# Cached-attention decode step: K and V loaded by whole batches of a cache head, score tiles of four batches in turn

## The chip, the cores and the metric

The kernel runs on one NeuronCore of one Trainium2 chip. The metric is device time in microseconds (us) of one execution; smaller is better. The kernel before was timed in three runs: median 1330.52 us, from 1330.09 to 1330.75. A further execution was profiled, and every row shown below comes from it.

## The reference

A decode step for 8 batches, one new token each, is the sum of three parts: the input `x`, attention over a long key and value cache, and a dense layer with the Mish activation. All data is float32.

```python
xn = layernorm(x)                                   # x: 8 x 512
q  = (xn @ wq) as 32 query heads of 128             # wq: 512 x 4096
s  = q . k_cache / sqrt(128)                        # k_cache: 8 batches x 8 heads x 8192 keys x 128
p  = softmax(s)                                     # 4 query heads share one cache head
o  = p . v_cache                                    # v_cache: the same shape as k_cache
A  = o @ wo                                         # wo: 4096 x 512
Bp = mish(xn @ w1 + b1) @ w2                        # w1: 512 x 1792, w2: 1792 x 512
out = x + A + Bp
```

The K cache and the V cache have 268.4 MB each. The four weights add 24.1 MB, so each execution reads 561 MB once, and nothing of it is used twice.

## The kernel before, in words

**Layout.** The host lays K and V out in blocks of 1024 keys, 512 KiB each, so that eight consecutive blocks hold the 8192 keys of one (batch, cache head). A K block is stored with the head dimension outermost, 128 rows of 1024 keys; a V block is stored so that each partition gets 1024 consecutive elements.

**Units.** Work on the cache goes by units of four blocks (`G` = 4), which is half of the keys of one (batch, head): 2 MiB. A unit is one DMA from the SyncE queue (`load_unit`, L94 to L101) into one of eight buffers named `kv` (L79, L85). The unit is read as 128 consecutive pieces, one for each partition, so each partition receives one contiguous row of 16 KiB. For K such a row is four consecutive head-dimension elements of one block: partition p holds block p // 32. Head 0 is loaded differently (L106 to L113), in rows of 8 KiB, two a partition, so that its query operand is smaller and ready sooner.

**Scores.** `scores` (L254 to L274) multiplies a K unit with a block-diagonal query operand `qT`: 128 columns, which are four blocks by 32 (4 query heads times 8 batches), with zeros outside the unit's own batch and block. The units of all eight batches accumulate into one PSUM tile of 128 x 1024, `S[0]` for the first half of the keys and `S[1]` for the second (L137). A unit takes eight matrix products of 128 x 128 by 512 columns, each of which the profile shows as two MATMUL records because the data is float32. After a half's last batch VectorE takes the row maximum (L272).

**Softmax and values.** After both halves of a head `maximum` (L278) and `weights` (L292) turn the maximum into a bias, ScalarE exponentiates each half out of PSUM (L303) and VectorE transposes it into `pt` (L304). `sums` (L314) adds up the row sums. `values` (L321) multiplies `pt` with V units, 16 columns wide, into one of two PSUM tiles `O`; after the second unit of a batch VectorE folds the result into `os` with four instructions (L337, L339), and `merge` (L350) sums over partitions with a small product. `outputs` (L363) multiplies a head's result with its part of `wo`.

**Projections.** A `wq` tile serves two heads: `project` (L201) makes the queries, scales and repeats them on VectorE (L219), transposes them four times on TensorE (L225) and copies them into `qc` (L228); `expand` (L235) writes `qc` into the block-diagonal `qT` with 16 small copies (L250).

**Order.** One list of items, `items` (L502 to L525), fixes the order: `wq`, then K units alone for the first head, then K units of head n+1 and V units of head n in turn, `wq` and `wo` tiles between them, and at the end 16 V units alone, the last `wo` tile and three `w2` tiles. The loop at L528 issues the load of the item that is six ahead (`AHEAD`), then the work of the present one. A load waits on the SyncE queue until its buffer is free. Small steps (softmax, merge, outputs) are put off by a count of items with `after` (L453), so that TensorE has other work while VectorE or ScalarE prepare them. The last of these, `outputs` of the last head, is put off by 0, so it is issued with the `wo` tile and before the `w2` tiles.

Of the kernel before, what the change touches and what calls it, by code (L numbers as in the profile page):

```python
# [8 lines left out]
F32 = mybir.dt.float32  # L9
# [16 lines left out]
UK = SK // NH  # L26
GK = UK // G
# [10 lines left out]
R = B * REP  # L38
PU = NH * B
# [4 lines left out]
KR = DH // Q  # L44
# [12 lines left out]
BUFS = 8  # L57
AHEAD = 6
# [3 lines left out]
def kernel(  # L62
# [21 lines left out]
    def buffer():  # L84
        return kv.tile([P, G * BW], F32, name="kv")  # L85
# [8 lines left out]
    def load_unit(src, n, b, s):  # L94

        lo = ((b * HKV + n) * NH + s) * G
        t = buffer()
        nc.sync.dma_start(
            t, src[lo : lo + G].rearrange("j p f -> (j p f)").rearrange("(p f) -> p f", p=P)
        )  # L100
        return t  # L101

    def load_k(n, b, s):
        if n > 0:
            return load_unit(kT, n, b, s)
        lo = ((b * HKV + n) * NH + s) * G  # L106
# [9 lines left out]
    def load_v(n, b, s):  # L116

        return load_unit(v, n, b, s)
# [18 lines left out]
    S = [psum.tile([P, GK], F32, name=f"s{i}") for i in range(NH)]  # L137
# [8 lines left out]

    rsel = const.tile([P, R], F32, name="rsel")

# [3 lines left out]
    qT = [const.tile([P, B * (QB + 1)], F32, name=f"qT{i}") for i in range(QBUFS)]  # L152
    qc = const.tile([P, HKV, KR, REP, B], F32, name="qc")
# [4 lines left out]
    def setup():  # L158
# [10 lines left out]
        scratch = work.tile([P, NH, GK], F32, name="e", bufs=1)  # L169
        xc, sq = scratch[:B, 0, :D], scratch[:B, 1, :D]  # L170
# [23 lines left out]
        )  # L194
        nc.vector.reduce_sum(rsel, ident.rearrange("p (g r) -> p r g", g=G), axis=AX.X)
        used = rsel[:, : W4 * REP]
        nc.vector.reduce_sum(hsel, used.rearrange("p (i h) -> p h i", h=REP), axis=AX.X)
        nc.vector.reduce_sum(isel, used.rearrange("p (i h) -> p i h", h=REP), axis=AX.X)


    def project(n, w):  # L201

        for c in range(CC):
            for h in range(REP):
                lo = (n % 2 * REP + h) * DH
                nc.tensor.matmul(  # L206
                    H[Q * h : Q * h + B, 384:512],
                    xnT[:, c, :],
                    w[:, c, lo : lo + DH],
                    start=(c == 0),  # L210
                    stop=(c == CC - 1),
                )

        k = KR if n > 0 else KA
        qs = work.tile([P, KR, P], F32, name="qs", bufs=1)[:, :k, :].rearrange(
            "p r (g i) -> p r g i", g=k
        )
        for g in range(k):
            nc.vector.tensor_scalar_mul(  # L219
                qs[:, :, g, :],  # L220
                H[:, 384:512].rearrange("p (i r) -> p r i", r=k),
                DH**-0.5,
            )
        for i in range(k):
            nc.tensor.transpose(  # L225
                H[:, i * P : (i + 1) * P], qs[:, i].rearrange("p g i -> p (g i)"), ident
            )
        nc.vector.tensor_copy(  # L228
            qc[:, n, :k],
            H[:, : k * P].rearrange("p (r h q) -> p r h q", r=k, h=REP)[:, :, :, :B],  # L230
        )

    Q0 = []

    def expand(n):  # L235

        if n > 0:
            k, cols, t = KR, P, qT[n % QBUFS]
        else:

            k, cols, t = KA, WK, work.tile([P, NH, W * R], F32, name="pt")
            t = t.rearrange("p s w -> p (s w)")[:, : B * (QA + 1)]
            nc.gpsimd.memset(t, 0.0)
            Q0.append(t)
        t = t.rearrange("p (b c) -> p c b", b=B)
        for g in range(k):
            rows = slice(P // k * g, P // k * (g + 1))
            for i in range(k):
                lo = i * cols + g * R
                nc.vector.tensor_copy(t[rows, lo : lo + R : B, :], qc[rows, n, i])  # L250

    NM = {}

    def scores(n, b, s, k):  # L254

        k_rows, cols, pitch, t = (KR, P, QB, qT[n % QBUFS]) if n > 0 else (KA, WK, QA, Q0[0])
        for c in range(GK // 512):
            for i in range(k_rows):
                w = pitch * b + cols * i
                at = i * BW + c * 512  # L260
                for j in range(P // cols):
                    nc.tensor.matmul(  # L262
                        S[s][cols * j : cols * (j + 1), c * 512 : (c + 1) * 512],
                        t[:, w : w + cols],
                        k[:, at : at + 512] if n > 0 else k[:, j, at : at + 512],
                        start=(b == 0 and i == 0),
                        stop=(b == B - 1 and i == k_rows - 1),
                    )
        if b == B - 1:
            if s == 0:  # L270
                NM[n] = work.tile([P, NH], F32, name="nm")
            nc.vector.tensor_reduce(  # L272
                NM[n][:, s : s + 1], S[s], axis=AX.X, op=ALU.max, negate=True
            )  # L274
# [3 lines left out]
    def maximum(n):  # L278

        nmb = work.tile([P, 1], F32, name="nmb")  # L280
        nc.vector.tensor_reduce(nmb, NM[n], axis=AX.X, op=ALU.min)
        nc.tensor.transpose(M[:1, 0:P], nmb, ident)
        nr = work.tile([1, Q], F32, name="nr")
# [3 lines left out]
        nx = NX[n] = work.tile([1, G, Q], F32, name="nx")  # L287
        nc.vector.tensor_copy(
            nx, nr.rearrange("p (o q) -> p o q", o=1).to_broadcast([1, G, Q])
        )  # L290

    def weights(n):  # L292


        nc.tensor.transpose(M[:, 128:129], NX[n].rearrange("p g q -> p (g q)"), ident[:1, :1])
        nmx = work.tile([P, 1], F32, name="nmx")
        nc.vector.tensor_copy(nmx, M[:, 128:129])  # L297
        e = work.tile([P, NH, GK], F32, name="e", bufs=1)
        l = work.tile([P, NH], F32, name="l")
        pt = PT[n] = work.tile([P, NH, W * R], F32, name="pt")  # L300
        m = W // TG
        for s in range(NH):
            nc.scalar.activation(e[:, s], S[s], AF.Exp, bias=nmx, accum_out=l[:, s : s + 1])  # L303
            nc.vector.transpose(  # L304
                pt[:, s].rearrange("p (m t r) -> p t m r", m=m, t=TG),
                e[:, s].rearrange("p (t q m) -> p t m q", t=TG, m=m),
            )
        ls = work.tile([P, 1], F32, name="ls")
        nc.vector.reduce_sum(ls, l, axis=AX.X)
        lsel = work.tile([P, R], F32, name="lsel")  # L310
        nc.vector.tensor_scalar(lsel, rsel, ls, None, op0=ALU.mult)
        return lsel

    def sums(n, lsel):  # L314
        nc.tensor.matmul(M[:, 136 : 136 + R], ones, lsel, start=True, stop=True)  # L315
        RT[n] = work.tile([P, REP, B], F32, name="r")
        nc.vector.reciprocal(RT[n].rearrange("p h b -> p (h b)"), M[:, 136 : 136 + R])  # L317
# [3 lines left out]
    def values(n, b, s, vt):  # L321
# [3 lines left out]
        for k in range(W // W4 // G):  # L325
            for c in range(G):
                j = G * k + c
# [252 lines left out]
```

## Time and profile before

| | |
|---|---|
| median of three runs | 1330.52 us |
| profiled execution | 1331.33 us |
| its span, first to last instruction | 1329.2 us |
| HBM read in it | 561.01 MB, 422 GB/s over the span |
| TensorE busy (matmul) | 1185.3 us, 89% of the span |
| VectorE, ScalarE, GpSimd busy | 200.8, 23.7, 8.7 us |
| mean granted TensorE clock | 0.972 |

The span leaves out 2.1 us of the profiled execution, before its first and after its last instruction. Matrix products are pipelined and their ends are modelled, so the time that a product costs in a stream is best read from the starts of two successive groups and not from the mean duration of one record. In the chain of work that ended last, the profile follows the program back from its last instruction, at each step to whatever released it; a piece named after a DMA is the time between the issue of that DMA and its landing.

### The profile page before, as it was taken

To read this page: it belongs to the slowest core of one execution; us is meant where nothing else is said; L and a number is where in the kernel's file an instruction comes from. 1 tells how busy PE (TensorE), PEld (TensorE's weight loads), DVE (VectorE), ACT (ScalarE), POOL (GpSimd) and SP (SyncE) were. 2 spreads that over 40 slices of the span, in tenths; PEclk is the share of its full clock that TensorE was granted. 3 is DMA by queue.
4 is the path that set the end of the run, shared out by engine and by line. 5 is a ranking of instruction groups with operands and counts; after the bars stand their busy time and mean duration, and the time that the engine had idled before them with its cause. 6 is when DMAs were issued, how large, how long until landed. Compare 5 with 4: busy or idle time off the path is not lost.

```text
span 1329.2 us, 11146 instructions
## 1 busy us (share of the span) xinstructions
PE 1185.3 (89%) x4962; PEld 457.6 (34%) x4962; DVE 200.8 (15%) x549; ACT 23.7 (2%) x39; POOL 8.7 (1%) x10
## 2 busy tenths in 40 slices
PE   5878999989999998989999999999999999999756
PEld 1223333333333333333333333433333333333212
DVE  4302020120002002030010200203100020100311
ACT  1000000000000000000000000000000000000000
POOL 2000000000000000000000000000000000000000
PEclk9999999999999999999999999899999999999786
DMA  9999999999999999999999999999999999999997
GB/s 383 421 424 428 428 424 427 427 428 430 426 428 426 429 426 426 426 426 429 427 427 427 427 428 424 429 426 427 427 428 427 428 427 428 427 428 427 427 428 298
DMA packets 44903, 561.80 MB, mean 423 GB/s; under 512 B 4396, under 2 KB 4528, under 8 KB 9784
## 3 DMA queue, kind: packets, MB, share of 16 engines
q1 hardware_dynamic: 44832, 561.07, 99.7%
q8 instruction: 39, 0.64, 0.2%
q14 instruction: 8, 0.07, 0.0%
q10 hardware_dynamic: 24, 0.02, 0.0%
HBM read 561.01 MB, written 0.07 MB: 422 GB/s over the span
## 4 chain that ended last, share of the span: by engine, by line
DMA 55%; PE 40%; DVE 3%; ACT 1%; issue 0%; ACTq 0%
DMA kv<-in_kT 50%; PE s L262 32%; PE o L328 6%; DMA kv<-in_w 3%; DMA kv<-in_v 2%; ACT e L303 1%; DVE os L339 1%; PE m L376 1%; PE h L442 0%; DVE e L173 0%; DVE os L337 0%; DVE nm L272 0%; PE h L206 0%; PE m L352 0%; PE m L315 0%
## 5 line engine op out<-in xcount | busy, mean ns | idle before, releaser
L262 PE MATMUL s<-kv,qT 128*128 128x512 f32 x1792 | 809.1, 605 | 44.9 <-DMA kv<-in_kT 41.6
L262 PEld LDWEIGHTS s<-kv,qT 128*128 128x128 f32 x1792 | 335.5, 192 | 506.5 <-issue 407.0
L328 PE MATMUL o<-kv,pt 128*16 128x512 f32 x2048 | 268.3, 630 | 13.1 <-DMA kv<-in_v 10.7
L337 DVE TENSOR_SCALAR os<-o,isel 128x128 f32<-128x128 f32 x64 | 22.5, 351 | 745.3 <-PE o L328 745.3
L328 PEld LDWEIGHTS o<-kv,pt 128*16 128x16 f32 x2048 | 55.1, 114 | 164.4 <-issue 139.6
L262 PE MATMUL s<-kv,pt 128*64 128x512 f32 x256 | 60.6, 619 | 14.1 <-DMA kv<-in_kT 14.1
L339 DVE SCALAR_TENSOR_TENSOR os<-o,isel,os 128x128 f32<-128x128 f32 x192 | 67.2, 350 | 6.3
L272 DVE TENSOR_REDUCE nm<-s 128x1 f32<-128x1024 f32 x16 | 19.6, 1225 | 216.1 <-PE s L262 215.9
L352 PE MATMUL m<-hsel,os 128*128 128x4 f32 x128 | 21.1, 235 | 31.2 <-DVE os L339 31.2
L352 PEld LDWEIGHTS m<-hsel,os 128*128 128x128 f32 x128 | 22.7, 193 | 67.0 <-DVE os L339 47.9
L303 ACT ACTIVATE e<-s,nmx 128x1024 f32<-128x1024 f32 x16 | 17.7, 1109 | 1174.5 <-DVE nmx L297 1174.5
L262 PEld LDWEIGHTS s<-kv,pt 128*64 128x64 f32 x256 | 17.7, 141 | 57.4 <-issue 32.2
L304 DVE STREAM_TRANSPOSE pt<-e 128x1024 f32<-128x1024 f32 x16 | 31.3, 2000 | 1.4 <-ACT e L303 1.3
L250 DVE COPY qT<-qc 32x32 f32<-32x32 f32 x112 | 16.1, 184 | 43.8 <-PE s L262 42.4
L206 PE MATMUL h<-kv,xnT 128*8 128x128 f32 x256 | 11.0, 327 | 4.0 <-DMA kv<-in_wq 2.2
L225 PE MATMUL h<-ident,qs 128*128 128x128 f32 x30 | 6.5, 348 | 7.8 <-DVE qs L219 7.8
L187 PE MATMUL m<-ident,e 8*128 8x8 f32 x4 | 0.6, 246 | 13.3 <-DVE e L185 13.3
L376 PE MATMUL m<-kv,oT 128*8 128x128 f32 x256 | 9.3, 291 | 3.0 <-DVE r L317 2.7
L206 PEld LDWEIGHTS h<-kv,xnT 128*8 128x8 f32 x256 | 7.1, 103 | 9.1 <-DMA kv<-in_wq 4.9
L317 DVE RECIPROCAL r<-m 128x32 f32<-128x32 f32 x8 | 2.9, 358 | 47.8 <-PE m L315 47.8
L376 PEld LDWEIGHTS m<-kv,oT 128*8 128x8 f32 x256 | 6.5, 94 | 4.3 <-DVE r L317 3.4
L442 PE MATMUL h<-kv,aT 128*8 128x128 f32 x112 | 6.0, 410 | 2.1 <-DMA kv<-in_w 2.1
(77 smaller groups left out, 89.5 us busy)
## 6 DMA issues: line engine op xcount, KB each, us to landing
kv<-in_kT SPq DMA_DIRECT2D x128, 2048.0 KB, 31.5
kv<-in_v SPq DMA_DIRECT2D x128, 2048.0 KB, 32.6
kv<-in_wq SPq DMA_DIRECT2D x4, 2048.0 KB, 28.9
kv<-in_wo SPq DMA_DIRECT2D x8, 1024.0 KB, 29.6
kv<-in_w SPq DMA_DIRECT2D x2, 1792.0 KB, 30.7
kv<-in_w SPq DMA_DIRECT2D x1, 2048.0 KB
kv<-in_w SPq DMA_DIRECT2D x1, 1024.0 KB, 30.7
kv<-in_w SPq DMA_DIRECT2D x1, 512.0 KB
```

The source lines that it names most:

```text
L206: nc.tensor.matmul(H[Q * h : Q * h + B, 384:512], xnT[:, c, :], w[:, c, lo : lo + DH], start=(c == 0), stop=(c == CC - 1),)
L225: nc.tensor.transpose(H[:, i * P : (i + 1) * P], qs[:, i].rearrange("p g i -> p (g i)"), ident)
L250: nc.vector.tensor_copy(t[rows, lo : lo + R : B, :], qc[rows, n, i])
L262: nc.tensor.matmul(S[s][cols * j : cols * (j + 1), c * 512 : (c + 1) * 512], t[:, w : w + cols], k[:, at : at + 512] if n > 0 else k[:, j, ...
L272: nc.vector.tensor_reduce(NM[n][:, s : s + 1], S[s], axis=AX.X, op=ALU.max, negate=True)
L303: nc.scalar.activation(e[:, s], S[s], AF.Exp, bias=nmx, accum_out=l[:, s : s + 1])
L304: nc.vector.transpose(pt[:, s].rearrange("p (m t r) -> p t m r", m=m, t=TG), e[:, s].rearrange("p (t q m) -> p t m q", t=TG, m=m),)
L328: nc.tensor.matmul(o[Q * c : Q * c + W4 * REP, :], PT[n][:, s, W4 * R * j + b : W4 * R * (j + 1) : B], vt[:, 512 * j : 512 * (j + 1)], sta ...
L337: nc.vector.tensor_scalar(os, o[:, :DH], isel[:, 0:1], None, op0=ALU.mult)
L339: nc.vector.scalar_tensor_tensor(os, o[:, DH * i : DH * (i + 1)], isel[:, i : i + 1], os, op0=ALU.mult, op1=ALU.add,)
L352: nc.tensor.matmul(M[:, 168 + b * REP : 168 + (b + 1) * REP], OS.pop((n, b)), hsel, start=True, stop=True)
L376: nc.tensor.matmul(M[Q * g : Q * g + B, 256:384], oT[n][:, h, :], w[:, h // 2, h % 2 * D + g * P : h % 2 * D + (g + 1) * P], start=(h == 0 ...
```

## The change

K and V tiles become whole (batch, head) pairs: eight blocks, 4 MiB, in one of four buffers of twice the size, with loads three items ahead. A K tile is read as 128 consecutive pieces of 32 KiB, so a partition holds eight consecutive head-dimension elements of one of eight blocks. A V tile is still laid out by halves, two rows of 16 KiB a partition in one DMA.

A matrix product now contracts over eight blocks of 16 partitions instead of four of 32. Its 128 output columns are four groups by 32, where 32 is 4 query heads times 2 halves times 4 batches. So one PSUM tile of 128 x 1024 holds the scores of a pack: four batches of one head, both halves. There are 16 packs, and pack p uses `S[p % 2]`. Softmax, sums and the scaling go by packs; the maxima of the two halves are combined in `maximum`. The first pack alone (four batches of head 0) is loaded in rows of 8 KiB.

The queries are spread by eight small products against `psel` instead of four transposes, and `expand` masks with `bsel` in eight VectorE instructions. `wo` comes in four tiles of 2 MiB instead of eight of 1 MiB, each for two heads, and `w1` in one tile instead of two. The work of an item is a generator now: it yields after every eight MATMUL records of a K tile, after the first half of a V tile and at its end, and the deferred steps count these yields instead of items.

```diff
...
-UK = SK // NH
-GK = UK // G
+GK = SK // (G * NH)
...
-R = B * REP
-PU = NH * B
-KR = DH // Q
+PB = 4
+NP = B // PB
+PACKS = HKV * NP
+U = NH * PB
+R = U * REP
+NB = G * NH
+KR = DH * NB // P
...
-BUFS = 8
-AHEAD = 6
+BUFS = 4
+AHEAD = 3
...
-        return kv.tile([P, G * BW], F32, name="kv")
+        return kv.tile([P, NB * BW], F32, name="kv")
...
+    def batch_blocks(src, p, b):
+        n, hb = divmod(p, NP)
+        lo = ((hb * PB + b) * HKV + n) * NB
+        return src[lo : lo + NB]
+    def load_k(p, b):
+        src = batch_blocks(kT, p, b)
         t = buffer()
-        nc.sync.dma_start(
-            t, src[lo : lo + G].rearrange("j p f -> (j p f)").rearrange("(p f) -> p f", p=P)
-        )
-        return t
-    def load_k(n, b, s):
-        if n > 0:
-            return load_unit(kT, n, b, s)
-        lo = ((b * HKV + n) * NH + s) * G
-        t = buffer().rearrange("p (j f) -> p j f", j=G // KA)
+        if p > 0:
+            nc.sync.dma_start(
+                t, src.rearrange("j p f -> (j p f)").rearrange("(p f) -> p f", p=P)
+            )
+            return t
+        t = t.rearrange("p (j f) -> p j f", j=NB // KA)
         nc.sync.dma_start(
             t,
-            kT[lo : lo + G]
-            .rearrange("(j a) p f -> j (a p f)", a=KA)
-            .rearrange("j (p f) -> p j f", p=P),
+            src.rearrange("(j a) p f -> j (a p f)", a=KA).rearrange("j (p f) -> p j f", p=P),
         )
         return t
+    def load_v(p, b):
+        t = buffer().rearrange("p (s f) -> p s f", s=NH)
+        nc.sync.dma_start(
+            t,
+            batch_blocks(v, p, b)
+            .rearrange("(s j) p f -> s (j p f)", s=NH)
+            .rearrange("s (p f) -> p s f", p=P),
+        )
+        return t
...
-    S = [psum.tile([P, GK], F32, name=f"s{i}") for i in range(NH)]
+    S = [psum.tile([P, GK], F32, name=f"s{i}") for i in range(2)]
...
+    def spread_q(k, copies, at, dst):
+        wide = DH // k
+        qs = work.tile([P, KR * P], F32, name="qs", bufs=1)[:, : k * P].rearrange(
+            "p (r g i) -> p r g i", r=k, g=copies
+        )
+        nc.vector.tensor_scalar_mul(
+            qs,
+            H[:, 384:512]
+            .rearrange("p (i r o) -> p r o i", r=k, o=1)
+            .to_broadcast([P, k, copies, wide]),
+            DH**-0.5,
+        )
+        for r in range(k):
+            nc.tensor.matmul(
+                H[:, at + r * R : at + (r + 1) * R],
+                qs[:, r].rearrange("p g i -> p (g i)"),
+                psel.rearrange("p h b -> p (h b)"),
+                start=True,
+                stop=True,
+            )
+        nc.vector.tensor_copy(
+            dst, H[:, at : at + k * R].rearrange("p (r h b) -> p r h b", r=k, h=REP)
+        )
...
+        if n == 0:
+            spread_q(KA, KA, KR * R, qc0)
+        spread_q(KR, NB, 0, qc[:, n % 4])
+    def expand(p):
+        n, hb = divmod(p, NP)
+        t = qT[p % QBUFS]
+        if p > 0:
+            t = t.rearrange("p (b c) -> p b c", b=PB)[:, :, :QB]
+            t = t.rearrange("p b (r q) -> p b r q", r=KR)
+            q = qc[:, n % 4, :, :, hb * PB : (hb + 1) * PB].rearrange("p r h b -> p b r h")
+            for j in range(NB):
+                s, g = divmod(j, G)
+                lo = g * R + s * PB
+                nc.vector.tensor_scalar(
+                    t[:, :, :, lo : lo + R - U + 1 : U], q, bsel[:, j : j + 1], None, op0=ALU.mult
+                )
+            return
...
+        t, sp = qT[p % QBUFS], S[p % 2]
...
+            else:
+                for r in range(KR):
+                    w = QB * b + P * r
+                    at = r * BW + c * 512
                     nc.tensor.matmul(
-                        S[s][cols * j : cols * (j + 1), c * 512 : (c + 1) * 512],
-                        t[:, w : w + cols],
-                        k[:, at : at + 512] if n > 0 else k[:, j, at : at + 512],
-                        start=(b == 0 and i == 0),
-                        stop=(b == B - 1 and i == k_rows - 1),
+                        sp[:, cols],
+                        t[:, w : w + P],
+                        k[:, at : at + 512],
+                        start=(b == 0 and r == 0),
+                        stop=(b == PB - 1 and r == KR - 1),
                     )
-        if b == B - 1:
-            if s == 0:
-                NM[n] = work.tile([P, NH], F32, name="nm")
-            nc.vector.tensor_reduce(
-                NM[n][:, s : s + 1], S[s], axis=AX.X, op=ALU.max, negate=True
-            )
+                    if r % 4 == 3 and (c, r) != (GK // 512 - 1, KR - 1):
+                        yield
+        if b == PB - 1:
+            NM[p] = work.tile([P, 1], F32, name="nm")
+            nc.vector.tensor_reduce(NM[p], sp, axis=AX.X, op=ALU.max, negate=True)
+            if p == 0:
+                nc.gpsimd.memset(t[:, : U * (QA + 1)], 0.0)...
+    def values(p, b, vt):
+        o = O[b % 2]
         for s in range(NH):
+            u = s * PB + b
+            for k in range(W // W4 // G):
+                for c in range(G):
+                    j = G * k + c
+                    nc.tensor.matmul(
+                        o[Q * c : Q * c + W4 * REP, :],
+                        PT[p][:, W4 * R * j + u : W4 * R * (j + 1) : U],
+                        vt[:, s, 512 * j : 512 * (j + 1)],
+                        start=(s == 0 and k == 0),
+                        stop=(s == NH - 1 and k == W // W4 // G - 1),
+                    )
+            if s == 0:
+                yield
...
+    def step():
+        for e in late:
+            e[0] -= 1
+        due = [f for k, f in late if k <= 0]
+        late[:] = [e for e in late if e[0] > 0]
+        for f in due:
+            f()
...
+    def k_work(p, b):
+        def work_on(t):
+            if (p, b) == (0, 0):
                 expand(0)
+            yield from scores(p, b, t)
+            if b == 0 and p + 1 < PACKS:
+                expand(p + 1)
+            if b == PB - 1:
+                def largest():
+                    maximum(p)
+                    after(1, exponents)
+                def exponents():
+                    lsel = weights(p)
+                    after(3 if p < PACKS - 1 else 2, lambda: sums(p, lsel))
+                after(3 if 0 < p < PACKS - 1 else 2, largest)
+            yield
+        return work_on
+    def v_work(p, b):
+        def work_on(t):
+            yield from values(p, b, t)
+            after(2, lambda: merge(p, b))
+            yield
+        return work_on
     def wo_work(n):
-        return lambda t: after(2 if n < HKV - 1 else 0, lambda: outputs(n, t))
+        def work_on(t):
+            after(3, lambda: outputs(n, t))
+            yield
+        return work_on
+    def w2_work(lo, hi):
+        def work_on(t):
+            down(lo, hi, t)
+            yield
+        return work_on
...
+    for i in range(PB * PACKS + PB):
+        p, b = divmod(i, PB)
+        if p < PACKS:
+            if b == 2 and p % (2 * NP) == 2 and p < PACKS - NP:
+                items.append(wq_item(p // (2 * NP) + 1))
+            if i == 2:
+                items.append((lambda: load_blocks(w1, 0, 2 * CC), w1_work))
+            items.append((lambda p=p, b=b: load_k(p, b), k_work(p, b)))
+        if p > 0:
+            items.append((lambda p=p, b=b: load_v(p - 1, b), v_work(p - 1, b)))
+            if i > PB and (i - PB + 1) % (2 * NP * PB) == 0:
+                n = (p - 1) // NP - 1
+                items.append((lambda n=n: load_blocks(wo, n * 2, 4), wo_work(n)))
...
-        items[i][1](tiles.pop(i))
-        due = [e for e in late if e[0] <= 0]
-        late[:] = [[k - 1, f] for k, f in late if k > 0]
-        for _, f in due:
-            f()
+        for _ in items[i][1](tiles.pop(i)):
+            step()
```

More of the change, by code (lines that the diff above doesn't have):

```diff
@@ L228, in project @@
[L228 to L250, printed above, removed]
+        if n == 0:
+            spread_q(KA, KA, KR * R, qc0)
@@ L404, in mish @@
                 )
[L406 to L407 removed]
+        scratch = [work.tile([P, GK], F32, name="e", bufs=2) for _ in range(2)]
+        h, a, z, z2 = (scratch[i // 2][:, i % 2 * 512 : i % 2 * 512 + FG] for i in range(4))
         nc.vector.tensor_copy(h, hp)
```

249 lines of the change are left out of this document (107 added, 142 removed).

## The prediction

> **What bounds the kernel now.** I read the page first: busy times, slices, DMA queues, and the head of the chain that ended last.
>
> ```profile
> PE 1185.3 (89%) x4962; PEld 457.6 (34%) x4962; DVE 200.8 (15%) x549; ACT 23.7 (2%) x39; POOL 8.7 (1%) x10
> ...
> GB/s 383 421 424 428 428 424 427 427 428 430 426 428 426 429 426 426 426 426 429 427 427 427 427 428 424 429 426 427 427 428 427 428 427 428 427 428 427 427 428 298
> DMA packets 44903, 561.80 MB, mean 423 GB/s; under 512 B 4396, under 2 KB 4528, under 8 KB 9784
> ...
> q1 hardware_dynamic: 44832, 561.07, 99.7%
> ...
> DMA 55%; PE 40%; DVE 3%; ACT 1%; issue 0%; ACTq 0%
> ...
> L262 PE MATMUL s<-kv,qT 128*128 128x512 f32 x1792 | 809.1, 605 | 44.9 <-DMA kv<-in_kT 41.6
> ...
> kv<-in_kT SPq DMA_DIRECT2D x128, 2048.0 KB, 31.5
> kv<-in_v SPq DMA_DIRECT2D x128, 2048.0 KB, 32.6
> ```
>
> The rate is flat at 424 to 430 GB/s from the fourth slice to the last but one: the transfers never pause, although the chain goes through PE for 40%. A tile lands 31.5 us after its issue, some six tiles of waiting data. So PE, wherever it is late, is late inside that reserve, and the end is set by the bytes, their rate and what follows the last of them. The bytes stay. The question is whether the rate changes, whether the reserve still holds, and what the tail does.
>
> Next, how far PE is from the bound: two pieces of the chain where PE works without a pause, and two where it waits.
>
> ```profile
> 128.16 6.97 PE s L262 x16
> 135.13 1.86 PE o L328 x16
> ...
> 427.41 1.21 ACT e L303 x2
> 428.67 8.57 PE s L262 x16
> ...
> 1027.07 7.15 PE s L262 x16
> 1034.23 31.97 DMA kv<-in_kT
> 1066.24 7.13 PE s L262 x16
> ```
>
> A K unit and a V unit cost PE 6.97 + 1.86 = 8.83 us. From 1027.07 to 1066.24, both begun by a landing, eight tiles arrive in 39.17 us, 9.79 a pair. PE has about 1 us of room a pair; the page's 41.6 us of waits for K, over seven heads, say that 5.9 us a head are left when all small steps are paid.
>
> Last, the rate by length of row. The windows show 3.5 KiB rows (`w1`, beside others), 8 KiB (K of head 0) and 16 KiB; the timeline shows single landings: K of head 0 from 48.74 to 88.61, and V of the last head.
>
> ```profile
> core 0: us, PE busy (x) PEld busy (x) DVE busy (x) ACT busy (x) POOL busy (x), PEclk, DMA share, GB/s
> 26.00:33.00 7.00, 7.00 (x30) 1.88 (x28) 0.00 (x0) 0.00 (x0) 0.00 (x0) 1.00 1.00 398
> 36.00:95.00 59.00, 46.18 (x226) 13.36 (x222) 11.68 (x16) 1.86 (x2) 0.00 (x0) 1.00 1.02 422
> 110.00:1300.00 1190.00, 1090.66 (x4385) 426.37 (x4388) 165.25 (x469) 16.10 (x28) 0.00 (x0) 0.98 1.01 427
> ```
>
> ```profile
> 48.74 3.65 PE L262 MATMUL s<-kv,pt 128*64 128x512 f32 x16 [0.87 <-DMA kv<-in_kT]
> 88.61 3.65 PE L262 MATMUL s<-kv,pt 128*64 128x512 f32 x16 [1.32 <-DMA kv<-in_kT]
> ...
> 1263.77 2.23 PE L328 MATMUL o<-kv,pt 128*16 128x512 f32 x16 [0.24 <-DMA kv<-in_v]
> 1302.94 3.62 PE L328 MATMUL o<-kv,pt 128*16 128x512 f32 x16 [1.75 <-DMA kv<-in_v]
> ```
>
> Eight tiles take 39.87 us in 8 KiB rows (4.984 each) and 39.17 in 16 KiB rows (4.896). Every engine is busy throughout, so shorter rows cost time on the engines themselves.
>
> **The price of a row.** A row is one packet. I count from the code: 240 tiles of 128 rows, 16 K tiles of 256, `wq` 4 x 512, `wo` 8 x 256, `w1` 2 x 512, `w2` 384, the output 128: 40,448. With one completion packet on each of 16 engines for 274 DMAs (4,384) that is 44,832, the queue's own number. Eight extra packets an engine cost 0.088 us by the landings, 11.0 ns each; by the windows (2 MiB at 422 and 427 GB/s: 4.970 and 4.911 us) 7.3 ns. I take 9.1, the middle.
>
> In the Trainium skill, "DMA: Bandwidth & Descriptors", section "Where 436 GB/s comes from", the ports allow 435.2 GB/s; a tile would need 4.819 us there, an estimate, and spread over nine packets the rest of 4.896 is 8.6 ns, with which the saving below would be 5.8 us. The landings agree with such a ceiling: none of the quoted rates passes it.
>
> **Part 1, the rows.** After the change: K 60 tiles of 128 rows and 4 of 512, V 64 of 256, the weights and output as before: 31,744, and 141 DMAs make 2,256 completions, 34,000 packets in all. So 8,704 fewer row packets, 544 an engine, and 133 fewer completions an engine. Rows: 544 x 9.1 ns = 5.0 us. Completions may cost nothing or as much as a row (1.2 us); I take half, 0.6. Saving 5.5 us (rounded). Bounds: 544 x 7.3 = 4.0 to 677 x 11.0 = 7.4. That a 32 KiB row costs no more than a 16 KiB one is not in the trace; the rivals take it up.
>
> **Part 2, PE work.** A 4 MiB K tile takes 2 x 8 products, 32 records, as two units do now: no change. Half of head 0 loses its cheap 64-column operand (3.65 against 6.97 us a unit, 8 units, 27 us more PE). The pack concerned runs in pairs with V like any other, so the room of 1 us a unit pair hides it. What grows is the projection:
>
> ```profile
> 17.66 1.90 PE L206 MATMUL h<-kv,xnT 128*8 128x128 f32 x32 [0.32 <-DVE qc L228]
> 19.62 0.89 DVE L219 TENSOR_SCALAR qs<-h 128x128 f32<-128x128 f32 x4 [2.02 <-PE h L206]
> 20.56 1.11 PE L225 MATMUL h<-ident,qs 128*128 128x128 f32 x4 [1.01 <-DVE qs L219]
> 21.71 0.29 DVE L228 COPY qc<-h 128x128 f32<-128x128 f32 x1 [1.21 <-PE h L225]
> ...
> L272 DVE TENSOR_REDUCE nm<-s 128x1 f32<-128x1024 f32 x16 | 19.6, 1225 | 216.1 <-PE s L262 215.9
> ...
> 1245.12 0.58 PE m L315 x2
> ```
>
> Now 4.3 us a head. After: 1.90; one spread of 1024 elements, between 1.2 us (a 1024-element read of PSUM at L272) and 2.2 (eight times 0.28, the 0.89 us being four that overlap); eight products of two records at 0.4 to 0.58 us (L315's pair); a copy of twice the size, at most 0.6. In all 6.6 to 9.3, so 2.3 to 5.0 us more a head. It fits into the 5.9 that are left, even less 0.7 a head for the faster stream, and costs nothing; without that cover it would be 18 to 40 us. `expand` (eight masked copies for sixteen, on VectorE alone) is priced at nothing: VectorE is 15% busy, and no one reads the operand before the next pack. The merges stay 64; they move two yields behind their `os`, which can only shorten PE's waits for VectorE.
>
> **Part 3, the turn of a head.** Today the first unit after a turn waits for ScalarE (1.21 us), which must leave `S`, and then takes 8.57 us for 7.06. With two tiles in turn the next pack writes the other one, so that wait goes. Nothing is gained at the end, because PE is not the bound there; next to be late is the K landing. There are 16 turns for 8.
>
> **Part 4, the reserve.** Four buffers of 4 MiB hold the same bytes, but come free in larger pieces. At a K landing three tiles are under way, 3 x 9.8 = 29 us; the K buffer is given back after 2 x 7.06 = 14.1 us of PE, when 15 us are still queued. What stands behind that waiting load on the SyncE queue are only later loads. At a projection (twice 9.3 us against 4.9 us of `wq` transfer, and a buffer that is only half full) I follow the landings: K at 0, V at 9.8, `wq` at 14.7, K at 24.4; PE does K to 14, V to 18, the projection to 36, K to 50, and the load issued then comes 3 us before the queue's last tile has landed. It holds, with the worst price. Cost 0.
>
> **Part 5, the tail.**
>
> ```profile
> 1312.77 1.93 PE L328 MATMUL o<-kv,pt 128*16 128x512 f32 x16 [0.44 <-DMA kv<-in_v]
> 1317.00 1.06 PE L376 MATMUL m<-kv,oT 128*8 128x128 f32 x32 [0.28 <-DVE oT L357]
> 1320.15 6.02 PE L442 MATMUL h<-kv,aT 128*8 128x128 f32 x112 [2.09 <-DMA kv<-in_w]
> 1326.25 0.29 DVE L540 TENSOR_TENSOR res<-h,acc 128x128 f32<-128x128 f32 x1 [7.83 <-PE h L442]
> ...
> 1320.00:1322.00 2.00, 1.85 (x36) 1.35 (x40) 0.00 (x0) 0.00 (x0) 0.00 (x0) 0.50 0.46 193
> 1324.00:1329.00 5.00, 2.17 (x44) 1.33 (x36) 0.29 (x1) 0.00 (x0) 0.00 (x0) 0.81 0.06 16
> ...
> 1246.13 1.90 PE m L376 x32
> ```
>
> Now `outputs` of the last head (32 records) is done before `w2` lands at 1320.15; then 112 records at a granted clock of 0.50 take 6.0 us, 54 ns each, longer than the 3.7 us in which the rest of `w2` arrives. After, `outputs` comes with a count of 3 and holds 64 records: yields of `wo`, the first and the second `w2` tile. So it runs between the second and third `down`, after `w2` has landed. At the low clock 64 records cost 64 x 59 ns = 3.8 us (1.90 for 32); at the full one 2.1 (1.06 for 32). The mean clock of 0.81 in the last 5 us means 0.50 until about 1325.9, 5.8 us after PE set in. By that, 96 `down` records take 5.2 us, `outputs` 0.55 low and 1.8 full, the last 16 at most 0.9: some 8.1 us against 6.0, +2.0. Bounds: all low, 9.9, +3.8; all warm, with every `down` waiting only for its tile, -0.3.
>
> In the Trainium skill, "TensorE: Matmul & The Clock Gate", Part 1, about 3.4 us of steady work lift the half clock; the tail would then cost 7.1 us, +1.0 for +2.0 (an estimate). The row at 0.50 from 1320 to 1322 agrees, the time until it rises here was longer.
>
> The start stays: `wq` is first in both, the first four loads go out without waiting, 14.2 MB or 33 us of transfer, and the first buffer returns before that: the two projections ended at 22.0 us here (21.71 + 0.29), and the first grows by at most 5.0, so by 27.
>
> **The sum.** -5.5 + 2.0 = -3.5 us. The profiled execution took 1331.33 (span 1329.2 and 2.1 around it), so 1327.8 in its terms; it stands 0.8 above the median of the runs, which gives 1327.0. About 0.2%, 2.7 us, is what a measurement here can tell from no change. Own range of this case: -7.4 - 0.3 to -4.0 + 3.8, so 1322.8 to 1330.3.
>
> **The rivals.**
> 1. *The longer rows bring nothing*: a 32 KiB row goes out as two packets, or costs in proportion. For: no row in the trace is longer than 16 KiB. Against: one packet a row, exactly, for five lengths. Then 60 x 8 packets an engine (4.4 us) come back: 1327.0 + 4.4 = 1331.4.
> 2. *The longer rows are slower* (other side). Place: the landing of a K tile. Partitions now start 32 KiB apart in memory, which no transfer here does. If K came at the rate of head 0's stage, 2 x 4.984 for 2 x 4.896 us, 60 tiles cost 10.6 us; only the 1.1 us of other packets are saved: 1330.5 + 10.6 - 1.1 + 2.0 = 1342. It decides from 9.82 us a K tile on (60 x 0.03 - 1.1 + 2.0 = 2.7). Against: 8 to 16 KiB went the other way. The Trainium skill, "DMA: Bandwidth & Descriptors", "Latency and other measured facts", reports rates that fall when the partitions' pitch is a large power of two, from 512 KiB on; no run here shows it.
> 3. *PE becomes the bound.* Each turn costs 1.21 + 1.5 us of lost pace plus its small products, some 3.5 us; if 16 turns cost that each, a head pays 3.5 more, with 5.0 for the projection 8.5 against 5.2 of room: 3.3 x 8 = 26, 1353. It decides from 5.2 us a head on. Against: the wait for `S` is gone and the steps are spread over yields.
>
> **Chances.** Forecast 0.62 (0.52 under 1327.9, 0.10 within 0.2%); rival 1, 0.17 (0.15 same, 0.02 slower with the long tail); rival 2, 0.12, and rival 3, 0.09, slower. So faster 0.52, same 0.25, slower 0.23. The range 1323 to 1335 holds the forecast, rival 1 and the mild ends of the others.
>
> **What would show it.** Part 1: 34,000 packets on the queue (41,680 by rival 1), and K landings of 9.7 us a tile. Parts 2 to 4: a flat rate up to the tail, waits for K that stay. Part 5: `outputs` between two `down` groups after `w2` lands. Wrong it would be with slices under 424 GB/s, K tiles above 9.82 us, or a chain that is all PE.

## The result, and the profile after

The changed kernel takes 1404.74 us, the median of four runs (1402.0 to 1405.57); the kernel before, beside it, 1330.6 us. The ratio is 1.055, with a 95% interval of 1.0536 to 1.0573: it is slower by 74 us, where the forecast was 1327.0 us, a little faster. The profiled execution has a span of 1403.8 us.

The page of the changed kernel, in the parts that answer those shown of before (busy times, slices, queue, chain by engine, three groups):

```profile
PE 1220.9 (87%) x5096; PEld 510.4 (36%) x5096; DVE 223.4 (16%) x620; ACT 24.6 (2%) x39; POOL 8.7 (1%) x10
...
GB/s 384 427 429 432 424 407 427 352 416 370 412 382 424 431 357 379 398 351 421 380 409 382 424 429 409 372 415 346 416 361 431 376 428 431 411 418 419 366 417 344
...
q1 hardware_dynamic: 34000, 561.06, 94.9%
...
PE 85%; DVE 11%; DMA 2%; ACT 1%; issue 1%; ACTq 0%
...
L313 PE MATMUL s<-kv,qT 128*128 128x512 f32 x1920 | 874.1, 615 | 0.0
L418 PE MATMUL m<-hsel,os 128*128 128x4 f32 x128 | 24.8, 264 | 97.6 <-DVE os L403 97.6
L374 PE MATMUL m<-lsel,ones 128*128 128x16 f32 x32 | 8.9, 357 | 46.2 <-DVE lsel L369 40.3
```

The rate was flat; now it falls to 346 to 382 GB/s in 13 of the 38 slices between the first and the last. The chain is PE for 85% and DMA for 2%, where it was 40% and 55%. The score products (L313) no longer wait for any K tile: 0.0 us of idle time, where 41.6 us were left. In their place the merges (L418) wait 97.6 us for `os`, and the sums (L374) 40.3 us for `lsel`. TensorE is the bound, with only 36 us more of busy time than before. The kernel before had this row for its merges (us in total, times, longest wait):

```profile
PE m L352 <- DVE os L339: 31.2, 23, 1.6
```

Where a pack spends its time is seen in the chain of the changed kernel, here one pack from 602.17 to 686.11 (start, duration, what):

```profile
602.17 15.23 PE s L313 x32
617.40 3.62 PE o L391 x32
621.04 0.36 DVE os L401
...
622.60 0.38 PE m L418 x2
622.99 13.84 PE s L313 x32
636.83 3.62 PE o L391 x32
...
642.42 13.84 PE s L313 x32
...
661.85 13.84 PE s L313 x32
675.68 3.62 PE o L391 x32
...
680.96 0.40 PE m L418 x2
...
681.61 0.23 PE m L356
...
682.12 1.21 ACT e L363 x2
683.36 1.97 DVE pt L364
...
685.50 0.61 PE m L374 x2
686.11 4.33 PE s L313 x5
```

Between a V tile and the next K tile stand 1.97 us (621.02 to 622.99): the four VectorE steps of `os`, and then the merge. At the turn of a pack it is 6.81 us (679.30 to 686.11): merge, bias, exponents, transposition and sums, one after the other, with the K tile behind them. The trace has 14 such turns; in three of them `outputs` stands among these steps too. The pack takes 56.75 us of scores, 14.48 of values, 3 x 1.97 and 6.81, together 83.9 us. Its transfers need 77.9 us, as the first experiment shows.

The code defers these steps into the next K tile. They were not executed there. The order of an engine's instructions is arranged when the program is built, by the compiler's planner, and the traces show that what came out is not the order of the code. The groups on TensorE as they follow each other in the two traces, with the number of products in each group (two records a product):

```
before                          after
L328 o<-kv,pt  x8               L391 o<-kv,pt   x16
L262 s<-kv,qT  x8               L418 m<-hsel,os        (merge)
L352 m<-hsel,os       (merge)   L313 s<-kv,qT   x16
L328 o<-kv,pt  x8               L391 o<-kv,pt   x16
L262 s<-kv,qT  x8               L418 m<-hsel,os        (merge)
```

Before, 39 of the 64 merges stand directly behind a K unit, so that VectorE has 7 us for `os`. After, not one stands behind a K tile.

### The profile page after: what moved, and what is told of

It reads as the page before. It is cut to its first block, busy times and chain, and to the rows that moved or that the text cites. A ratio compares the mean times of both kernels' runs of the same rounds, so it can differ in the third digit from the quotient of the medians.

```text
span 1403.8 us, 11230 instructions
## 1 busy us (share of the span) xinstructions
PE 1220.9 (87%) x5096; PEld 510.4 (36%) x5096; DVE 223.4 (16%) x620; ACT 24.6 (2%) x39; POOL 8.7 (1%) x10
## 4 chain that ended last, share of the span: by engine, by line
PE 85%; DVE 11%; DMA 2%; ACT 1%; issue 1%; ACTq 0%
PE s L313 62%; PE o L391 17%; DVE os L403 4%; DVE pt L364 2%; PE h L235 2%; PE m L418 2%; DVE os L401 2%; DMA kv<-in_kT 1%; ACT e L363 1%; PE s L301 1%; DVE qs L227 1%; DMA kv<-in_w 1%; PE m L374 1%; PE h L251 1%; DVE e L188 0%
## 5 line engine op out<-in xcount | busy, mean ns | idle before, releaser
L313 PE MATMUL s<-kv,qT 128*128 128x512 f32 x1920 | 874.1, 615 | 0.0
L313 PEld LDWEIGHTS s<-kv,qT 128*128 128x128 f32 x1920 | 374.2, 198 | 452.4 <-issue 452.4
L391 PE MATMUL o<-kv,pt 128*16 128x512 f32 x2048 | 235.2, 599 | 0.0
L418 PE MATMUL m<-hsel,os 128*128 128x4 f32 x128 | 24.8, 264 | 97.6 <-DVE os L403 97.6
L418 PEld LDWEIGHTS m<-hsel,os 128*128 128x128 f32 x128 | 19.3, 190 | 142.2 <-DVE os L403 142.2
L374 PE MATMUL m<-lsel,ones 128*128 128x16 f32 x32 | 8.9, 357 | 46.2 <-DVE lsel L369 40.3
L235 PE MATMUL h<-psel,qs 128*128 128x32 f32 x132 | 24.4, 351 | 11.9 <-DVE qs L227 11.9
L274 DVE TENSOR_SCALAR qT<-qc,bsel 128x128 f32<-128x128 f32 x120 | 31.6, 343 | 0.1
L301 PE MATMUL s<-kv,qT 128*64 128x512 f32 x128 | 29.8, 624 | 1.7 <-DMA kv<-in_kT 1.7
L235 PEld LDWEIGHTS h<-psel,qs 128*128 128x128 f32 x132 | 23.3, 273 | 14.9 <-DVE qs L227 14.9
L374 PEld LDWEIGHTS m<-lsel,ones 128*128 128x128 f32 x32 | 7.2, 281 | 49.1 <-DVE lsel L369 41.3
L301 PEld LDWEIGHTS s<-kv,qT 128*64 128x64 f32 x128 | 9.2, 144 | 22.8 <-issue 20.2
L227 DVE TENSOR_SCALAR qs<-h 128x1024 f32<-128x1024 f32 (+1 forms) x9 | 10.2, 1131 | 6.6 <-PE h L251 6.6
```

The source lines that it names most:

```text
L235: nc.tensor.matmul(H[:, at + r * R : at + (r + 1) * R], qs[:, r].rearrange("p g i -> p (g i)"), psel.rearrange("p h b -> p (h b)"), start= ...
L274: nc.vector.tensor_scalar(t[:, :, :, lo : lo + R - U + 1 : U], q, bsel[:, j : j + 1], None, op0=ALU.mult)
L301: nc.tensor.matmul(sp[WK * z : WK * (z + 1), cols], t[:, w : w + WK], k[:, NH * s + z, at : at + 512], start=(b == 0 and s == 0 and i == 0 ...
L313: nc.tensor.matmul(sp[:, cols], t[:, w : w + P], k[:, at : at + 512], start=(b == 0 and r == 0), stop=(b == PB - 1 and r == KR - 1),)
L374: nc.tensor.matmul(M[:, 136 : 136 + n], ones, lsel.rearrange("p h b -> p (h b)"), start=True, stop=True)
L391: nc.tensor.matmul(o[Q * c : Q * c + W4 * REP, :], PT[p][:, W4 * R * j + u : W4 * R * (j + 1) : U], vt[:, s, 512 * j : 512 * (j + 1)], sta ...
```

## The experiments

Theory A: the order on TensorE's queue is the cause; the small steps wait there for VectorE and ScalarE ahead of a K tile that has landed, which makes TensorE longer than the transfers. Theory B: four large buffers come free too late, so the transfers stop whatever the order is. Times are medians; each ratio is to the kernel before, run beside it.

### Every deferred step tied to its place

```diff
     def step():
...
         for f in due:
-            f()
+            pe = the last TensorE instruction traced so far
+            with tc.issue_after(pe):
+                f()
```

The tie is there to set the order in TensorE's queue; the work and the loads are the same.

> Every deferred step is tied in TensorE's queue behind the product group after which the code defers it; nothing else differs from the changed kernel. Theory A (the order on TensorE: small steps stand ahead of the next K tile and TensorE waits for VectorE and ScalarE there): a pair falls from 19.43 us (602.17 + ... to 642.42 to 661.85) to 13.84 + 3.62 + 0.39 = 17.85 us, below the 19.5 us of its transfers, so the transfers are the bound again: 1324 to 1331 us, rate flat near 429 GB/s, no wait of TensorE for os. Theory B (four buffers of 4 MiB come free too late, whatever the order): the rate keeps its dips and the time stays at 1390 us or more.

Measured: 1326.21 us, ratio 0.997 (0.9957 to 0.9983). The slices of this kernel, and its chain in the middle:

```profile
GB/s 383 426 433 424 432 428 427 432 427 428 432 424 430 433 424 432 430 425 433 431 425 430 429 427 426 429 431 432 429 428 425 423 430 431 429 430 431 427 427 300
```

```profile
608.34 24.58 DMA kv<-in_kT
...
633.05 3.67 PE s L313 x8
636.73 0.12 PE m L418 x2
...
647.62 24.33 DMA kv<-in_kT
...
672.00 3.70 PE s L313 x8
```

The rate is flat again and the chain goes through the K landings. Two pairs of tiles arrive in 38.95 us (633.05 to 672.00), 77.9 a pack. A merge costs 0.12 us on the chain, and follows the first eight records without a pause. Theory A holds; theory B, with the same buffers, falls. The page of the changed kernel pointed that way already: its score products waited 0.0 us for K tiles, and tiles that come too late would have made them wait. The 78.5 us by which the untied kernel is longer compare with 14 packs x 6.0 us = 84; the difference, with the first pack, the projections and the 2 MiB tiles between, was not taken apart.

### Only the merges, and only the turn

```diff
-            after(2, lambda: merge(p, b))
+            after(2, lambda: behind(lambda: merge(p, b)))
```

Here `behind` is the tie of the first experiment.

> Only the merges are tied behind the first eight records of the next K tile; the steps of a pack's turn stay as compiled. Theory A: four merge waits of 1.6 us go from each pack of some 84 us, 77.6 us are left, about the 78 us of the transfers; the projections (10 to 12 us, three times) come on top: 1328 to 1345 us. The waits for lsel stay near 40 us or move. Theory B: no change, 1390 us or more.

Measured: 1324.39 us (ratio 0.9956, 0.9939 to 0.9973), better than expected. In the built program the merges are in the K tile, and the bias, exponents and sums, which stand behind the last merge, have moved into it too. So this run does not price the merges alone.

```diff
-                    after(1, exponents)
+                    after(1, lambda: behind(exponents))
```

and likewise for `largest` and `sums`.

> Only the steps of a pack's turn (maximum, exponents, sums) are tied; the merges stay ahead of the K tile. Theory A: the turn loses some 5 us of waiting and 1.4 us of lower clock, 15 times, so 84 becomes about 78 us a pack, equal to the transfers: 1330 to 1350 us; the merge waits of 97.6 us stay. Theory B: no change.

Measured: 1343.01 us (ratio 1.010, 1.0075 to 1.0126), as expected. In the trace the bias product still stands ahead of the K tile, with the merge; at the turns only the sums have moved, behind the tile, so that the exponents and the transposition run beside it. Of the waits of this kernel, the one for `lsel` is gone and this one is left:

```profile
PE m L418 <- DVE os L403: 97.2, 61, 1.6
```

So the turn accounts for 61.7 us of the excess, and the merges for the last 16.8, counted in this order. The two are not independent: with the turn taken away first the pack is close to the transfers' 77.9 us, and the merges can then gain only what is left. That the merges, taken away first, would do the same is an estimate (83.9 - 4 x 1.6 = 77.5); no run shows it.

### The row of 32 KiB alone

```diff
             nc.sync.dma_start(
-                t, src.rearrange("j p f -> (j p f)").rearrange("(p f) -> p f", p=P)
+                t.rearrange("p (s f) -> p s f", s=NH),
+                src.rearrange("(s j) p f -> s (j p f)", s=NH).rearrange("s (p f) -> p s f", p=P),
             )
```

> As with every step tied, but K tiles after the first pack are read as two rows of 16 KiB a partition, as V is (the elements then stand elsewhere in the tile, so the scores are not the reference's; the work is the same). It prices the longer row alone. By the prediction's price of a packet (9.1 ns) 60 tiles x 8 packets an engine are 4.4 us more than with rows of 32 KiB; 0 if a long row costs as much as two, and less than with long rows if these are slower. Packets on the queue: 41,680 for 34,000.

Measured: 1330.86 us, 4.65 us more than with long rows (1326.21). The queue and a long window of this kernel, and then the same window with long rows:

```profile
q1 hardware_dynamic: 41680, 561.06, 99.6%
```

```profile
110.00:1300.00 1190.00, 1096.24 (x4444) 456.62 (x4446) 184.22 (x524) 18.08 (x30) 0.00 (x0) 0.97 1.01 427
```

```profile
110.00:1300.00 1190.00, 1099.91 (x4469) 456.78 (x4471) 184.27 (x524) 18.07 (x30) 0.00 (x0) 0.97 1.01 429
```

The last column is GB/s. 480 packets an engine cost 4.65 us, 9.7 ns each. The long row brings what the prediction counted on (4.4 us), and neither of the rivals about rows holds.

### The bad order in the kernel before, and the good one

```diff
-                after(1, lambda: merge(n, b))
+                merge(n, b)
+                merged.append(last_pe())
...
+            with tc.issue_after(merged.pop()):
                 scores(n, b, s, t)
```

> The kernel before, with one thing of the changed one: each merge stands in TensorE's queue right behind the V unit that ends a batch and ahead of the next K unit. If the order is what costs (theory A), some 41 merges more wait 1.4 to 1.6 us for os, about 60 us of TensorE time over seven heads that had 41.6 us left: 1335 to 1350 us, and little of the wait for K remains. If the size of the tiles is what costs (theory B), small tiles bear this order: 1330 to 1332 us.

Measured: 1355.17 us (ratio 1.0189, 1.0174 to 1.0204), somewhat beyond the expected 1350. All 64 merges now wait, for 23 before. Of the waits for K, which were 55.8 us in the kernel before, little is left:

```profile
PE m L352 <- DVE os L339: 103.2, 64, 1.6
...
PE s L262 <- DMA kv<-in_kT: 15.4, 12, 1.3
```

These 15.4 us are all waits of head 0, whose K units come alone; the score products of the other seven heads, which had 41.6 us left, wait for no K unit any more. So the place of the merges alone makes the kernel with 2 MiB units slower too, by 24.6 us, with neither large tiles nor few buffers: TensorE has become its bound. The order of the turn's steps was not tried in this kernel.

```diff
         for _, f in due:
-            f()
+            with tc.issue_after(the last TensorE instruction):
+                f()
```

> The kernel before, with its deferred steps tied where its code defers them, as in the kernel with every step tied. The waits for os (31.2 us) go or nearly so. Theory A: the transfers are the bound there already, so 1329 to 1332 us, the time moves into waits for K. If tying were a gain by itself, whatever the bound, some 20 us less.

Measured: 1330.41 us, ratio 1.000 (0.9991 to 1.001). The waits for `os` fall from 31.2 to 7.9 us, the waits for K rise. The row of the kernel before, and then the two of this one:

```profile
PE s L262 <- DMA kv<-in_kT: 55.8, 67, 2.1
```

```profile
PE s L262 <- DMA kv<-in_kT: 70.8, 85, 1.9
...
PE m L352 <- DVE os L339: 7.9, 8, 1.6
```

Where the transfers are the bound, better order on TensorE is worth nothing; it only widens the room.

### K in two DMAs, order left to the planner

```diff
+            rows = src.rearrange("j p f -> (j p f)").rearrange("(p f) -> p f", p=P)
+            for i in range(2):
+                cols = slice(i * NB // 2 * BW, (i + 1) * NB // 2 * BW)
+                nc.sync.dma_start(t[:, cols], rows[:, cols])
```

> The changed kernel, nothing tied, but each K tile comes by two DMAs of 2 MiB, half of every row each (16 KiB pieces, 32 KiB apart). As compiled, the steps of a turn now stand inside the next K tile and the merges still ahead of it, so theory A expects the time of the kernel with the turn tied alone, 1340 to 1350 us, 0 to 5 more for the shorter rows where the transfers bind. If pieces that start 32 KiB apart were read slower, the rate in its best slices would be under the 427 GB/s of 16 KiB rows.

Measured: 1378.63 us (ratio 1.0357, 1.0333 to 1.038): faster than the changed kernel, but not the 1340 to 1350 expected. Only part of the turn moved. The sums stand inside the next K tile now, so that the exponents and the transposition run beside its first eight records; the bias still stands ahead of the tile, with the last merge. The maximum stands right behind the last K tile of a pack, ahead of its V tile, and waits for VectorE there. From the chain of this kernel:

```profile
647.10 13.85 PE s L314 x32
660.98 1.24 DVE nm L325
...
662.25 0.27 PE m L334
662.52 3.62 PE o L392 x32
```

A pack takes 81.8 us (592.25 to 674.06 in this chain), 3.9 more than its transfers. That the planner places steps by when it reckons a tile to have arrived is a guess: it fits this run, since smaller transfers changed the place of some steps, but the run does not show how it reckons, and that stays open.

### The tail, the rows of V, and three buffers

With every step tied, the last `outputs` runs between two `down` groups. The ends of the first two experiments' chains, the first with every step tied, the second with the merges alone:

```profile
1314.86 4.47 PE h L509 x96
1319.34 1.75 PE m L443 x64
1321.08 0.48 PE h L509 x16
```

```profile
1317.24 1.04 PE h L509 x27
...
1318.59 0.85 PE h L509 x21
```

Untied, `outputs` was done before `w2` landed, and the span is 1322.2 us for 1324.3. So:

```diff
-            after(3, lambda: outputs(n, t))
+            after(3 if n < HKV - 2 else 1, lambda: outputs(n, t))
```

> Every step tied, and the last outputs deferred by one yield instead of three, so that they run before w2 lands. The tail from the landing of w2 took 6.7 us with 64 records of outputs inside it, 4.7 us where they stood before it: 2.0 us less than with every step tied, 1323 to 1325 us.

Measured: 1324.93 us (ratio 0.9958, 0.9943 to 0.9973), 1.3 us less than with every step tied, in the direction expected and somewhat short of the 2.0.

The price of a row was then used once more, on V. In the device code only the load changes; the host lays the keys of each K block out in the order in which the V rows now come.

```diff
-        t = buffer().rearrange("p (s f) -> p s f", s=NH)
         nc.sync.dma_start(
-            t,
-            batch_blocks(v, p, b)
-            .rearrange("(s j) p f -> s (j p f)", s=NH)
-            .rearrange("s (p f) -> p s f", p=P),
+            t, batch_blocks(v, p, b).rearrange("j p f -> (j p f)").rearrange("(p f) -> p f", p=P)
         )
```

> As with every step tied and the last outputs early, and V tiles too come in one row of 32 KiB a partition; the host lays the keys of a K block out in the order that the V rows then have, which leaves the softmax sum the same. By the price measured for K rows (4.65 us for 60 tiles of 8 packets an engine fewer) 64 V tiles save 5.0 us: 1319 to 1321 us, 25,808 packets on the queue. If the price holds for K alone: 1324 to 1325.

Measured: 1319.69 us, ratio 0.9921 (0.9905 to 0.9938): the fastest of all, ahead of both kernels. 512 packets an engine fewer saved 5.24 us, 10.2 ns each. Its queue and its long window:

```profile
q1 hardware_dynamic: 25808, 561.06, 99.5%
```

```profile
110.00:1300.00 1190.00, 1099.80 (x4473) 457.15 (x4471) 185.70 (x528) 18.07 (x30) 0.00 (x0) 0.97 1.00 430
```

Last, the reserve:

```diff
-BUFS = 4
-AHEAD = 3
+BUFS = 3
+AHEAD = 2
```

> Every step tied, three buffers of 4 MiB for four, loads two items ahead. It tells what the reserve of four was worth. At a K landing two tiles are under way, 19.5 us, and the K buffer returns after 14 us: 5 us are left in steady pairs, so the transfers hold there; at the projections (10 to 12 us) and behind 2 MiB tiles the queue runs empty for some us, 3 to 7 times: 1330 to 1350 us. If four buffers were as good as empty in that kernel, three would cost far more, 1380 us and up.

Measured: 1375.43 us (ratio 1.0341, 1.0324 to 1.0358), 49 us more than with four, worse than expected. The slices of this kernel dip more often than its three later projections explain:

```profile
GB/s 386 352 422 417 431 392 404 433 426 424 427 390 368 427 425 396 385 428 430 422 418 367 402 434 412 401 389 424 430 432 420 337 431 426 433 427 423 424 428 309
```

Four buffers are enough with the good order, and one fewer is not. So the number of buffers can bind, as theory B has it, but with four it does not. Why steady pairs suffer too was not settled.

## Why the prediction was wrong, point by point

**Part 1, the rows: right.** 34,000 packets, exactly. The saving on K rows was taken as 4.4 us, by 9.1 ns a packet; it measured 4.65, and 9.7 ns. Rivals 1 and 2 are out, and a pair of tiles lands every 19.5 us with every step tied, 9.7 a tile, as the prediction said. The Trainium skill's warning in "DMA: Bandwidth & Descriptors", "Latency and other measured facts", on large power-of-two pitches does not reach here: pieces 32 KiB apart ran at 428 to 432 GB/s in the best slices of the kernel with two DMAs a tile; its 512 KiB was not tried.

**Part 2, PE work: wrong, and this is the step that failed.** The prediction said that the merges "move two yields behind their `os`, which can only shorten PE's waits for VectorE". It took the order written in the code for the order on the engine's queue. The merges came to stand ahead of the K tile instead of inside it, and their waits went from 31.2 to 97.6 us. The trace of before held the warning, in its chain:

```profile
124.28 1.90 PE o L328 x16
126.21 0.36 DVE os L337
...
127.77 0.39 PE m L352 x2
```

The code puts a merge off by one item, behind the next K unit, yet here it stands directly behind its own V unit and waits for `os`, and the K unit follows at 128.16. It is one of 13 merges of that trace that stand directly ahead of a K unit. Read against the code, these rows say that the written order does not bind. The growth of the projections was the smaller matter. From the last V product to the next K product the three later projections of two heads, with one merge among each, take 9.1 to 12.5 us in the changed kernel, for 6.7 to 8.2 before, some 1.7 us more a head where the prediction had 2.3 to 5.0; and the room was there for it, since with the order tied the transfers bind.

**Part 3, the turn: wrong for the same reason.** The exponents no longer have to leave `S` for the next pack, as the prediction said, but the next pack's first K tile stood behind the sums in the queue instead, and so behind the whole sequence: 6.81 us in the pack shown, at 14 turns. "There are 16 turns for 8" was noted and given no price.

**Part 4, the reserve: held.** With the order tied, the rate is flat with four buffers. A K tile lands 24.6 us after its issue (median), 14.9 more than its own 9.7, for the 15 us that the prediction reckoned to be still queued. By the packet records of that trace the least that was still queued when a load went out, between 110 and 1290 us, was 4.6 us, for the 3 us reckoned at a projection. The run with three buffers shows that a reserve one tile smaller does not do.

**Part 5, the tail: right in kind, too large in size.** With the written order `outputs` did run between the `down` groups. From the landing of `w2` to the last addition it took 6.73 us (1314.86 to 1321.59) for 6.10 before, +0.6 instead of +2.0, because the clock was low for a shorter time: 0.71 was granted over 1314.86 to 1317.0, 0.50 to 1319.1 and 0.98 from there. So 96 `down` records took 4.47 us for the 5.2 of the prediction, and the 64 of `outputs` 1.75 for 2.35. In the changed kernel itself the planner had put `outputs` ahead of the `down` groups.

**The sum.** With the order that the prediction assumed, the kernel takes 1326.21 us; the forecast was 1327.0. That it is so close is partly luck: with the tail as measured the sum would have been 1325.6. For the changed kernel as built, the signs that the prediction named for being wrong are there: slices under 424 GB/s, and a chain that is PE for 85%. TensorE did become the bound, as rival 3 had it with its chance of 0.09, but only in part for the reason that it gave. Its price, 1353, counted 3.5 us more a head for the turns and 5.0 for the projections. Measured, a pack spends 14.1 us on what is neither scores nor values at full pace (83.9 less 4 x 17.46): 8.2 at the turn (6.81, and 1.39 of lower clock), the rest at the three other merges; the rival left the merges out. That is 6.0 us over the transfers, 12 us a head where the rival had 3.3.

## What to carry to other kernels

A deferred step in the code is a wish; what counts is the place of the instruction in its engine's queue, and that can be read from the trace (which group ran directly behind which) before any price is set. When an engine runs at nine tenths of the bound, list each small step that stands in its queue ahead of large work, with what it waits for, and tie it where it matters. And price each change of a row's length by packets: here some 10 ns for each packet an engine, the same from 16 to 32 KiB for K and for V.

## What the runs showed of the hardware

In these runs the price of a packet does not grow with the row: 7.3 to 11.0 ns were read between rows of 8 and 16 KiB, and 9.7 and 10.2 ns were measured between 16 and 32 KiB.

A turn costs more than its wait. Windows of the changed kernel around a turn, where the last three columns are granted clock, DMA share and GB/s:

```profile
590.00:597.00 7.00, 5.51 (x38) 1.44 (x36) 4.82 (x18) 0.00 (x0) 0.00 (x0) 1.00 1.02 431
597.00:602.00 5.00, 1.04 (x5) 0.87 (x6) 2.52 (x5) 1.21 (x2) 0.00 (x0) 0.60 0.99 426
602.00:604.00 2.00, 2.00 (x4) 0.97 (x5) 0.26 (x1) 0.00 (x0) 0.00 (x0) 0.50 0.97 418
604.00:606.00 2.00, 2.00 (x5) 0.84 (x4) 0.00 (x0) 0.00 (x0) 0.00 (x0) 0.79 1.05 451
```

After 5 us with 1.04 us of matrix work the granted clock is 0.50 for the first 2 us of the next K tile, which then takes 15.23 us for 13.84. The clock is back some 3.3 us after work resumed at 601.56 (0.79 over 604 to 606 is 0.50 until about 604.8); in the tail of the kernel before it took 5.8 us. It fell at about 598.0 (0.60 over 597 to 602), 2.6 us after the last value product. The 451 GB/s of the last row is no rate that the engines hold: its DMA share of 1.05 shows that 2 us are too short for one.

The Trainium skill, "TensorE: Matmul & The Clock Gate", Part 1, lets the clock rise after at least one busy window of about 3.4 us and fall after at least one idle window, and says that the windows run free of the kernel. From that, the next full window ends 3.4 to 6.8 us after work begins (an estimate). The rise in the two traces, 3.3 and 5.8 us, agrees with it to 0.1 us; the fall came sooner than a whole idle window.
